# A ConvNeXt V2 block on one core: x turned by the DMA, the convolution cut into 32x32 tiles, a third of its result copied out by VectorE

## The chip, the core and the metric

The kernel runs on one core of one Trainium2 chip. A core has a matrix engine (TensorE, in the profile PE, with its weight loads as PEld), three elementwise engines (VectorE = DVE, ScalarE = ACT, GpSimd = POOL), and a queue for transfers (SyncE = SP); sixteen DMA engines move data. Each engine works through its own list of instructions in order, and lists are tied together by semaphores. Matrix results land in PSUM, eight banks of 512 float32 columns on 128 partitions; everything else lies in SBUF, also 128 partitions. The metric is the device time of one execution in microseconds.

## The reference

```python
# x (1,512,512,96), dw (3,3,96), w1 (96,384), w2 (384,96), gamma/beta (384): bfloat16
for i in range(3):
    for j in range(3):
        out = out + xp[:, i:i+H, j:j+W, :] * dw[i, j]      # depthwise 3x3, xp is x with a border of zeros
h = layernorm(out)                                         # over the 96 channels, eps 1e-5
h = gelu(einsum('bhwc,ce->bhwe', h, w1))                   # 96 -> 384 channels
gx = sqrt((h * h).sum(axis=(1, 2)) + 1e-6)                 # one number per channel, over the whole image
nx = gx / (gx.mean(axis=-1) + 1e-6)
h = gamma * (h * nx) + beta + h
return x + einsum('bhwe,ec->bhwc', h, w2)                  # 384 -> 96 channels
```

The sum over the image stands between the two products: nothing of the output can be made before all of h has been seen. The kernel therefore makes two passes over the image.

## The kernel before

The image is cut into 128 blocks of four rows (GR = 4), 2048 pixels each.

**First pass.** One slot of the loop at L826 does one block's convolution and, some slots later, the same block's norm and product. For block b:
- `load_x` (L216, queue SP) brings the block in with 16 pixels and a pixel of overlap at either side in each partition; `turn_x` (L442, two VectorE transposes of 128x576) puts channels on partitions, in the ring `xT` of five blocks. It is called three slots ahead of use, the load four.
- `conv_taps` (L463) makes the 3x3 convolution as matrix products with diagonal weights `Wq`. The partitions of a third `i` of the channels hold four image rows of 32 channels; an instruction takes 64 partitions (two rows) and gives 32 (one output row), so a block is 72 matmuls of 511 or 512 columns, in three bursts of 24. In a burst, eight successive matmuls go to the eight different 64x32 parts of the array. The result lies in banks 4 to 6 (`Y3`); in some early slots in others (`spare`).
- `evac` (L496) copies it to SBUF (`y_bf`) with one ScalarE instruction of 1536 columns. The next block's first burst writes the same banks and has to wait for it.
- POOL squares `y_bf` and later multiplies it with the row of 1/sigma (`yn`); PE sums for the moments (`stage_stats`), SP writes `yn` to DRAM and reads it back as `ynT` with 96 channels on the partitions.
- `mlp_units` (L699) makes h for an older block in 12 pieces of 512 columns: PE multiplies with `w1p`, ScalarE applies gelu into `g`. A block has four quarters. In `cm_quads(b)` of them h has its channels on the partitions, and three VectorE BATCH_NORM_STATS2 per quarter gather the sum of squares. The other quarters have pixels on the partitions, and PE gathers the squares by twelve 128x128 products per quarter (`gram`). Blocks with q % 10 in (0, 3, 7) below 114 are *whole*: four quarters with channels on the partitions, and `g` is stored to DRAM by SP. The block after a whole one has two such quarters, the others three; the last sixteen that are neither whole nor held have two or one.

The order is written out by hand: every engine call goes through `InOrder`, which keeps program order, so an engine's list is the order of the source. A slot with a product reads: burst 0, units 0 to 2, squares, burst 1, `turn_x`, units 3 to 5, squares, gram, units 6 and 7, squares, burst 2, `evac`, gram, units 8 to 11 and the moments. SP's list in a slot: the load of x for four slots later, the read of `ynT`, four writes of `yn`, rows and broadcasts of 1/sigma, and one third of a stored `g`.

**Tail.** The last 14 blocks have only their products left (`mlp_tail`, L672).

**Second pass** (from the middle of L950 on). For every block, h is loaded, kept or made again; 16 products per quarter with the scaled `W2s` give the output, VectorE adds x (`stage_mm2`, L328), SP stores.

Of the kernel before, what the change touches and what calls it, by code (L numbers as in the profile page):

```python
# [8 lines left out]
ALU = mybir.AluOpType  # L9
# [3 lines left out]
GR = 4  # L13
# [43 lines left out]
def kernel(  # L57
# [42 lines left out]
    def cm_quads(q):  # L100
        if is_whole(q) or is_held(q):
            return NQ
        if q > HELD[0]:
            return 1
        return 2 if q >= NBLK - 16 or (q - 1) % 10 in WHOLE else 3
# [4 lines left out]
    def chans(i):  # L110
        return slice(i, 64, 2) if i < 2 else slice(64, 96)
# [4 lines left out]
    def quad(flat_ap, t):  # L116
        return flat_ap.rearrange("p r (t g m) -> p t g r m", t=NQ, m=MB)[:, t]

    def quad_out(flat_ap):
        return flat_ap.rearrange("p (g r m) -> p g r m", r=GR, m=MB)  # L120
# [20 lines left out]
    Wq = consts.tile([128, NI, 3, GR, 32], bf16, name="Wq")  # L141
# [41 lines left out]
    SL = PXP + 2  # L183
    with ExitStack() as p1:
# [25 lines left out]
        xinpool = pc.enter_context(tc.tile_pool(name="xin", side="right", bufs=4))  # L210
        xins = {}

        def shift(h, j):
            return 1 if (h, j) == (0, GR - 1) else -1 if (h, j) == (1, 0) else 0

        def load_x(b):  # L216
            t = xinpool.tile([128, SL, C], bf16, name="xin")
            off = x.offset + b * GR * W * C
            rows = lambda p0, p1, s0, s1: (
                t[p0:p1, s0:s1, :].rearrange("p g c -> p (g c)"),  # L220
                bass.AP(x.tensor, off + (p0 * PXP - 1 + s0) * C, [[PXP * C, p1 - p0], [1, (s1 - s0) * C]]))
            if b == 0:
                pool.memset(t[0:1, 0, :], 0.0)
                parts = [(16, 128, 0, SL), (0, 16, 1, SL), (1, 16, 0, 1)]
            elif b == NBLK - 1:
                pool.memset(t[96:128, SL - 1, :], 0.0)
                parts = [(0, 112, 0, SL), (112, 128, 0, SL - 1), (112, 127, SL - 1, SL)]
            else:
                parts = [(0, 128, 0, SL)]
            for part in parts:  # L230
                o, i_ = rows(*part)
                sp.dma_start(out=o, in_=i_)
            xins[b] = t

        Wd = gpool.tile([128, NQ, NCH, QW], bf16, name="g")[:].rearrange("p t j w -> p (t j w)")[
            :, :NI * 9 * 32].rearrange("p (i k c) -> p i k c", i=NI, k=9)
# [8 lines left out]
        act.activation(out=Wq[:].rearrange("p i d j c -> p (i d j c)").rearrange("p (a w) -> p a w", a=3),  # L245
                       in_=zrow[:, None, :NI * GR * 32].to_broadcast([128, 3, NI * GR * 32]), func=ACTF.Identity)
# [8 lines left out]
        xtpool = pc.enter_context(tc.tile_pool(name="xt", side="right", bufs=1))  # L255
# [6 lines left out]
        NXT = 5  # L262
        xt_ring = []
        xt_all = xtpool.tile([128, NXT, NI, SL * MB], bf16, name="xT")
        for i in range(NXT):
            xt_ring.append(xt_all[:, i])
        assert NXT * NI * SL * MB >= NQ * NCH * QW
        g_over = xt_all[:].rearrange("p x i s -> p (x i s)")[:, :NQ * NCH * QW].rearrange(
            "p (t j w) -> p t j w", t=NQ, j=NCH)
# [32 lines left out]
        def cm_unit(g, ynt, t):  # L302
            U = banks3()
            for j in range(NCH):
                pe.matmul(quad_out(U[:, j, :]), lhsT=w1p[:, j * 128:(j + 1) * 128],
                          rhs=quad(ynt[:], t), start=True, stop=True)
            act.activation(out=g[:, t, :, :], in_=U, func=ACTF.Gelu_apprx_tanh)

        def px_unit(g, ynt, t):
            Uf = banks3().rearrange("p k w -> p (k w)")  # L310
            for r in range(GR):
                c = r * E
                while c < (r + 1) * E:
                    sz = min((r + 1) * E - c, W - c % W)
                    pe.matmul(Uf[:, c:c + sz], lhsT=ynt[:, r, t * 128:t * 128 + 128],
                              rhs=w1p[:, c - r * E:c - r * E + sz], start=True, stop=True)
                    c += sz
            act.activation(out=g[:, t, :, :].rearrange("p j w -> p (j w)"), in_=Uf, func=ACTF.Gelu_apprx_tanh)
# [9 lines left out]
        def stage_mm2(n, q):  # L328
            g, xb = grp[q]["g"], grp[q]["xb"]
            GQ = QW // 128  # L330
            o_sb = late.o.tile([128, PXP, C], bf16, name="o_sb")
            for sub in range(NSUB):
                O = out_bank()
                for gl_ in range(GPS):
                    gg = sub * GPS + gl_
                    for j in range(NCH):
# [3 lines left out]
                dve.tensor_tensor(out=o_sb[:, sub * GPS:(sub + 1) * GPS, :], in0=O,  # L340
                                   in1=xb[:, sub * GPS:(sub + 1) * GPS, :], op=ALU.add)
# [57 lines left out]
        n = 0  # L399
        for h in range(2):  # L400
            for j in range(GR):
                for q in (2 * h, 2 * h + 1):
                    a = q + GR * shift(h, j) - j + 1
                    if 0 <= a < 3:
                        n += 1
                        o, i_ = Wq[32 * q:32 * q + 32, :, :, j, :], Wd[32 * q:32 * q + 32, :, 3 * a:3 * a + 3, :]
                        if n % 2:
                            act.activation(out=o, in_=i_, func=ACTF.Identity)
                        elif n % 4:
                            dve.tensor_copy(out=o, in_=i_)  # L410
                        else:
                            pool.tensor_copy(out=o, in_=i_)

# [28 lines left out]
        def turn_x(b):  # L442
            xin = xins.pop(b)
            t = xt_ring[b % NXT]
            pairs = t[:, 0:2, :].rearrange("p i s -> p (i s)").bitcast(f32)
            dve.transpose(out=pairs.rearrange("p (g m) -> p g m", m=MB),
                          in_=xin[:, :, 0:64].bitcast(f32))
            dve.transpose(out=t[:, 2, :].rearrange("p (g m) -> p g m", m=MB), in_=xin[:, :, 64:96])

        def x_rows(b, p0, p1, i, c0, n):  # L450
            t = xt_ring[b % NXT]
            if i == 2:
                return t[p0:p1, 2, c0:c0 + n]
            return t[p0:p1, 0:2, :].rearrange("p i s -> p (i s)").rearrange(
                "p (s e) -> p s e", e=2)[:, c0:c0 + n, i]

# [6 lines left out]
        def conv_taps(b, spare):  # L463
# [6 lines left out]
            for n in range(3):  # L470
                mms.append([(h, j, (n + h) % NI, dx) for dx in (0, -1, 1) for j in range(GR) for h in range(2)])
            flat = [m for ms in mms for m in ms]
            first = {}
            last = {}
            for n, (h, j, i, dx) in enumerate(flat):
                first.setdefault((i, j), n)
                last[i, j] = n

            def burst(n, fence=True):
                k = sum(len(ms) for ms in mms[:n])  # L480
                for h, j, i, dx in mms[n]:
                    src = b + shift(h, j)
                    o0, o1 = max(0, -dx), W - max(0, dx)
                    pe.matmul(
                        Y[i][32 * j:32 * j + 32, o0:o1],
                        lhsT=Wq[64 * h:64 * h + 64, i, dx + 1, j, :],
                        rhs=x_rows(src, 64 * h, 64 * h + 64, i, MB * (1 + dx) + o0, o1 - o0)
                        if 0 <= src < NBLK else zrow[64 * h:64 * h + 64, o0:o1],
                        start=first[i, j] == k,
                        stop=last[i, j] == k,  # L490
                    )
# [207 lines left out]
        def mlp_units(b):  # L699
# [5 lines left out]
            def cm_mm(dst, j, t):  # L705
                pe.matmul(quad_out(dst), lhsT=w1p[:, j * 128:(j + 1) * 128], rhs=quad(yt[:], t), start=True, stop=True)

            def unit(bank, n):
# [10 lines left out]
                while c < end:  # L719
# [4 lines left out]
                    else:  # L724
# [3 lines left out]
                        col = (cm_quads(b) + t) * 128  # L728
                        pe.matmul(Uf[:, c - c0:c - c0 + sz], lhsT=yt[:, r, col:col + 128], rhs=w1p[:, e0:e0 + sz],
# [93 lines left out]
        turn_x(0)  # L823
        turn_x(1)
        turn_x(2)
        for s in range(last_slot + 1):  # L826
# [34 lines left out]
            elif not mlp:  # L861
                if s + 3 < NBLK:
                    turn_x(s + 3)
# [21 lines left out]
            else:  # L885
# [10 lines left out]
                if s + 3 < NBLK:  # L896
                    turn_x(s + 3)
# [100 lines left out]
    with p2:  # L998
        def out_part(q, o_sb, sub):
# [3 lines left out]
                    "(p g) c -> p g c", g=PXP)[:, sub * GPS:(sub + 1) * GPS],  # L1003
                in_=o_sb[:, sub * GPS:(sub + 1) * GPS])
# [47 lines left out]
```

## Time and profile before

| | us |
|---|---|
| median of 3 runs | 1489.95 (1483.42 to 1490.06) |
| the profiled execution: time / span of the profile | 1482.67 / 1480.8 |
| start and first slots | 0 to 113 |
| first pass, a product in every slot | 113 to 884 |
| last 14 products | 884 to 980 |
| end of the sums, second pass | 980 to 1481 |

Granted TensorE clock: 0.994 of full. The page gives each engine's busy share, then the span in 40 slices, the DMA queues, the chain that ended last, and groups of like instructions. A group's line reads: source line (most are that of the helper, L35), engine, operation, output and inputs by the program's names, partitions x elements, how many | busy time together, mean duration of one | idle time of the engine ahead of them and what ended it. As instructions of one engine overlap, mean times count can exceed the busy time. A timeline's line is start, length of the merged group, engine, operation, and in brackets the idle time ahead of it.

### The profile page before, as it was taken

The page shows a single profiled execution, that of the slowest core. Times are in us where ns is not written, and L with a number is a line of the kernel's source. Part 1 is how long each engine was busy: PE and PEld are TensorE (multiplying, and loading weights), DVE is VectorE, ACT ScalarE, POOL GpSimd, SP SyncE. Part 2 cuts the span into 40 slices and gives each one's busy share as a digit, 9 for nine tenths or more (in the row PEclk, how much of TensorE's full clock was granted, in tenths as well). Part 3 has the DMA queues.
Part 4 walks back from the last instruction along what each step waited for, and adds up shares of the span by engine and source line. Part 5 has one row for each costly group of instructions (what it writes and reads, how often), then busy time and mean ns, then how long its engine had stood idle before and what let it go on. Part 6 is the DMA issues. An engine that isn't in the chain of part 4 may idle for free.

```text
span 1480.8 us, 54225 instructions
## 1 busy us (share of the span) xinstructions
PE 1391.3 (94%) x23125; PEld 810.4 (55%) x23125; DVE 1182.0 (80%) x2135; ACT 1414.4 (96%) x1595; POOL 1300.3 (88%) x922
## 2 busy tenths in 40 slices
PE   8888999999999999999999997789999999999998
PEld 3434444444444444444444445467777777776776
DVE  7849989999999999999999987965555555555555
ACT  7888989999999999999999999999999999999997
POOL 3459889998998999998999987569999999999997
PEclk9999999999999999999999999999999999999999
DMA  5568788788888888888888866669999999999997
GB/s 180 179 205 255 241 253 280 228 271 260 260 248 264 258 264 255 276 253 254 263 258 266 263 216 195 195 225 409 366 359 402 417 416 413 419 410 417 411 412 282
DMA packets 167768, 433.08 MB, mean 292 GB/s; under 512 B 31558, under 2 KB 81318, under 8 KB 163046
## 3 DMA queue, kind: packets, MB, share of 16 engines
q1 hardware_dynamic: 151284, 326.04, 66.3%
q0 software_dynamic: 14880, 103.43, 17.6%
q8 instruction: 181, 2.97, 0.8%
q14 instruction: 61, 0.50, 0.1%
q10 hardware_dynamic: 1362, 0.15, 0.1%
HBM read 273.30 MB, written 156.22 MB: 290 GB/s over the span
## 4 chain that ended last, share of the span: by engine, by line
PE 30%; ACT 24%; DMA 19%; POOL 13%; DVE 6%; issue 4%; SPq 4%; POOLq 0%; ACTq 0%; DVEq 0%
PE PS L35 30%; ACT g L35 16%; DMA out_dram<-o_sb 9%; POOL yn L35 6%; ACT y_bf L35 5%; POOL ysq L35 5%; SPq L35 4%; DMA yn_dram<-yn 3%; DVE bst L35 3%; DMA xin<-in_x_dram 2%; DMA rbc<-r_dram 2%; DMA ynT<-yn_dram 1%; DMA g_dram<-g 1%; DVE o_sb L35 1%; ACT xT L35 1%
## 5 line engine op out<-in xcount | busy, mean ns | idle before, releaser
L35 ACT ACTIVATE g<-PS 128x512 bf16<-128x512 f32 (+2 forms) x1062 | 727.7, 864 | 16.5 <-PE PS L35 15.6
L35 DVE BATCH_NORM_STATS2 bst<-g 128x6 f32<-128x512 bf16 x1110 | 671.3, 672 | 35.4 <-ACT g L35 34.5
L35 PE MATMUL PS<-ynT,w1p 128*128 128x512 bf16 x2181 | 609.6, 381 | 23.6 <-ACT g L35 5.4
L35 ACT ACTIVATE gr<-PS 128x1536 bf16<-128x1536 f32 x360 | 498.5, 1459 | 18.8 <-PE PS L35 13.8
L35 POOL TENSOR_TENSOR yn<-y_bf,rbc 128x1536 bf16<-128x1536 bf16 x126 | 391.3, 3108 | 77.3 <-ACT rbc L35 21.9
L35 DVE TENSOR_TENSOR o_sb<-PS,xb 128x384 bf16<-128x384 f32 x512 | 277.3, 556 | 227.0 <-PE PS L35 190.1
L324 POOL TENSOR_TENSOR xb<-xr,B2c 128x1536 f32<-128x1536 bf16 x118 | 368.1, 3133 | 4.3 <-DVE o_sb L35 2.0
L35 PE MATMUL PS<-xT,Wq 64*32 64x511 bf16 (+1 forms) x9198 | 340.5, 389 | 26.2 <-ACT y_bf L35 8.1
L35 POOL TENSOR_TENSOR ysq<-y_bf 128x1536 bf16<-128x1536 bf16 x114 | 313.6, 2752 | 12.8 <-ACT y_bf L35 12.8
L35 PEld LDWEIGHTS <-w1p 128*128 128x128 bf16 x2181 | 171.6, 98 | 222.0 <-issue 133.4
L35 PEld LDWEIGHTS <-gr 128*128 128x128 bf16 x4296 | 212.1, 98 | 68.9 <-issue 12.0
L35 PE MATMUL PS<-W2s,gr 128*128 128x96 bf16 x4224 | 223.5, 206 | 8.2 <-DVE o_sb L35 8.0
L35 PEld LDWEIGHTS <-Wq 64*32 64x32 bf16 x9216 | 111.9, 90 | 193.3 <-issue 145.9
L35 ACT ACTIVATE y_bf<-PS 128x1536 bf16<-128x1536 f32 (+2 forms) x135 | 199.4, 1482 | 17.4 <-PE PS L35 13.3
L35 DVE STREAM_TRANSPOSE xT<-xin 128x576 f32<-128x576 f32 (+1 forms) x256 | 181.4, 748 | 8.1 <-DMA xin<-in_x_dram 8.1
L35 PEld LDWEIGHTS <-g 128*128 128x128 bf16 x1704 | 104.9, 98 | 86.3 <-issue 54.3
L35 PE MATMUL PS<-w1p,ynT 128*128 128x256 bf16 (+2 forms) x822 | 125.8, 273 | 8.0 <-ACT xT L35 3.2
L35 PE MATMUL PS<-g 128*128 128x128 bf16 x1464 | 122.6, 220 | 2.9 <-DVE PS L35 2.6
L35 PEld LDWEIGHTS <-gl 128*128 128x128 bf16 x1680 | 82.8, 98 | 26.8 <-issue 5.0
L35 PE MATMUL PS<-W2s,gl 128*128 128x96 bf16 x1680 | 89.5, 206 | 3.4 <-DVE o_sb L35 3.2
L35 PEld LDWEIGHTS <-ynT 128*128 128x128 bf16 x822 | 64.1, 97 | 31.5 <-issue 13.7
L279 POOL DMA_DIRECT2D xr<-in_x_dram x115 | 63.7, 555 | 14.2 <-POOL xb L324 14.2
(105 smaller groups left out, 576.5 us busy)
## 6 DMA issues: line engine op xcount, KB each, us to landing
xin<-in_x_dram SPq DMA_DIRECT2D x126, 432.0 KB
g_dram<-g SPq DMA_DIRECT2D x105, 512.0 KB
gl<-g_dram POOLq DMA_DIRECT2D x35, 1536.0 KB, 11.3
yn_dram<-yn SPq DMA_DIRECT2D x512, 96.0 KB
ynT<-yn_dram SPq DMA_DIRECT2D x128, 384.0 KB
out_dram<-o_sb SPq DMA_DIRECT2D x127, 384.0 KB
xr<-in_x_dram POOLq DMA_DIRECT2D x123, 384.0 KB, 6.9
ynT<-yn_dram SPq DMA_DIRECT2D x85, 512.0 KB
```

Source lines behind the costliest of these rows:

```text
L35: r = f(*a, **k)
L279: pq.dma_start(out=xr[:], in_=x[0, r0:r0 + GR].rearrange("r w c -> (r w) c").rearrange("(p g) c -> p g c", g=PXP))
L324: pq.tensor_tensor(out=xb[:], in0=grp[q]["xr"][:], in1=bias[:, None, :].to_broadcast([128, PXP, C]), op=ALU.add)
```

## The change

Six things, all in the first pass but the fourth.
1. x is loaded by a DMA that transposes (2-byte elements, 128 x 1536 to 128 x 12 x 128), straight into one ring of six blocks; the loads with overlap, the VectorE transposes and the copies of the weights at the start go. An element's partition is now given by its channel within 32 and by q % 4 with q = 3 (w mod 16) + i for column w and third i; the row and the rest of the column run along the free dimension. A quarter of a block is the pixels with one value of w mod 4.
2. The convolution takes 32 partitions and gives 32. Each of the nine taps is 12 matmuls of 512 columns on 12 of the sixteen 32x32 parts of the array. With dx of -1 or 1 one of the four column groups has its neighbour in another 16-pixel piece: its 512 columns are cut into 384 and 124, two matmuls on the same part of the array, one right behind the other, three such pairs per tap. For dx = -1 the pair stands first of the four of a third, for dx = 1 last. Where the ring wraps (every sixth block, above or below) each of a tap's matmuls is cut once more. In all 17892 matmuls of the convolution stand where 9216 did.
3. The bursts are now one dx each, with all three dy: 36, 45 and 45 matmuls.
4. The quarter of the product and of the output is one contiguous run on the product's side, and every fourth pixel in the second pass' addition and in the last block's four stores.
5. ScalarE copies out two thirds (1024 columns) and VectorE one (512).
6. The 34 blocks after a whole one have three quarters with channels on the partitions in place of two.

```diff
--- before
+++ after
@@ cm_quads @@
-        return 2 if q >= NBLK - 16 or (q - 1) % 10 in WHOLE else 3
+        return 2 if q >= NBLK - 16 else 3
@@ chans, quad @@
-        return slice(i, 64, 2) if i < 2 else slice(64, 96)
+        return slice(32 * i, 32 * i + 32)
-        return flat_ap.rearrange("p r (t g m) -> p t g r m", t=NQ, m=MB)[:, t]
+        return flat_ap[:, t, :]
@@ weights of the convolution @@
-    Wq = consts.tile([128, NI, 3, GR, 32], bf16, name="Wq")
+    Wd = consts.tile([128, NI, 9, 32], bf16, name="Wd")
@@ load_x @@
-        xinpool = pc.enter_context(tc.tile_pool(name="xin", side="right", bufs=4))
+        NXT = 6
+        xtpool = pc.enter_context(tc.tile_pool(name="xt", side="right", bufs=1))
+        xt = xtpool.tile([128, GR, NI, NXT * 128], bf16, name="xT")
         def load_x(b):
-            t = xinpool.tile([128, SL, C], bf16, name="xin")
...
-                sp.dma_start(out=o, in_=i_)
-            xins[b] = t
+            c = b % NXT * 128
+            sp.dma_start(out=xt[:, :, :, c:c + 128].rearrange("p k a s -> p (k a) s"),
+                         in_=x[0, b * GR:(b + 1) * GR].rearrange("r w c -> (r w c)").rearrange(
+                             "(p e) -> p e", p=128), transpose=True)
@@ stage_mm2 @@
-                dve.tensor_tensor(out=o_sb[:, sub * GPS:(sub + 1) * GPS, :], in0=O,
-                                   in1=xb[:, sub * GPS:(sub + 1) * GPS, :], op=ALU.add)
+                dve.tensor_tensor(out=o_sb[:, sub::NQ, :], in0=O, in1=xb[:, sub::NQ, :], op=ALU.add)
@@ setup: the loop that copies Wd into Wq (6 copies on ACT, 3 on DVE, 3 on POOL) goes, and turn_x with its calls @@
-            dve.transpose(out=pairs.rearrange("p (g m) -> p g m", m=MB),
-                          in_=xin[:, :, 0:64].bitcast(f32))
-            dve.transpose(out=t[:, 2, :].rearrange("p (g m) -> p g m", m=MB), in_=xin[:, :, 64:96])
@@ conv_taps @@
-            for n in range(3):
-                mms.append([(h, j, (n + h) % NI, dx) for dx in (0, -1, 1) for j in range(GR) for h in range(2)])
+            for dx in (0, -1, 1):
+                mm = []
+                for dy in (0, -1, 1):
+                    runs = []
+                    for r in range(GR):
+                        row = b * GR + r + dy
+                        if 0 <= row < H:
+                            at_ = row % (NXT * GR) * MB
+                            if runs and runs[-1][1] + (r - runs[-1][0]) * MB == at_:
+                                runs[-1][2] += 1
+                            else:
+                                runs.append([r, at_, 1])
+                    for r, at_, nr in runs:
+                        o = slice(r * MB, (r + nr) * MB)
+                        for i in range(NI):
+                            for sx in range(GR):
+                                wrap = not 0 <= sx + dx < GR
+                                q = NI * ((sx + dx) % GR) + i
+                                ko, ki = slice(0, GR), slice(0, GR)
+                                if wrap:
+                                    ko, ki = (slice(1, GR), slice(0, GR - 1)) if dx < 0 else (
+                                        slice(0, GR - 1), slice(1, GR))
+                                yo = Y[i][32 * sx:32 * sx + 32, :].rearrange("p (k s) -> p k s", k=GR)
+                                xi = xt[32 * (q % 4):32 * (q % 4) + 32, :, q // 4, :]
+                                w = Wd[32 * (q % 4):32 * (q % 4) + 32, i, 3 * (dy + 1) + dx + 1, :]
+                                mm.append(((i, sx), w, yo[:, ko, o], xi[:, ki, at_:at_ + nr * MB]))
+                                if wrap:
+                                    k0, k1 = (0, GR - 1) if dx < 0 else (GR - 1, 0)
+                                    m0, m1 = (1, 0) if dx < 0 else (0, 1)
+                                    mm.append(((i, sx), w,
+                                               yo[:, k0, o].rearrange("p (r m) -> p r m", m=MB)[:, :, m0:m0 + MB - 1],
+                                               xi[:, k1, at_:at_ + nr * MB].rearrange(
+                                                   "p (r m) -> p r m", m=MB)[:, :, m1:m1 + MB - 1]))
+                mms.append(mm)
@@ evac @@
-                    act.activation(out=y[:, 2, :], in_=Ub[:, 0, :], func=ACTF.Identity)
+                    dve.tensor_copy(out=y[:, 2, :], in_=Ub[:, 0, :])
-                    act.activation(out=y[:], in_=Y3, func=ACTF.Identity)
+                    act.activation(out=y[:, 0:2, :], in_=Y3[:, 0:2, :], func=ACTF.Identity)
+                    dve.tensor_copy(out=y[:, 2, :], in_=Y3[:, 2, :])
@@ out_part (last block only) @@
-                    "(p g) c -> p g c", g=PXP)[:, sub * GPS:(sub + 1) * GPS],
-                in_=o_sb[:, sub * GPS:(sub + 1) * GPS])
+                    "(p g) c -> p g c", g=PXP)[:, sub::NQ],
+                in_=o_sb[:, sub::NQ, :])
```

More of the change, by code (lines that the diff above doesn't have):

```diff
@@ L116, in quad @@
     def quad(flat_ap, t):
-        return flat_ap.rearrange("p r (t g m) -> p t g r m", t=NQ, m=MB)[:, t]
-    def quad_out(flat_ap):
-        return flat_ap.rearrange("p (g r m) -> p g r m", r=GR, m=MB)
+        return flat_ap[:, t, :]
     def yn_src(q):
@@ L182 @@
     p2 = ExitStack()
-    SL = PXP + 2
     with ExitStack() as p1:
@@ L209 @@
         pc = p1.enter_context(ExitStack())
-        xinpool = pc.enter_context(tc.tile_pool(name="xin", side="right", bufs=4))
-        xins = {}
-        def shift(h, j):
-            return 1 if (h, j) == (0, GR - 1) else -1 if (h, j) == (1, 0) else 0
-        def load_x(b):
-            t = xinpool.tile([128, SL, C], bf16, name="xin")
[L218 to L231, printed above, removed]
-                sp.dma_start(out=o, in_=i_)
-            xins[b] = t
-        Wd = gpool.tile([128, NQ, NCH, QW], bf16, name="g")[:].rearrange("p t j w -> p (t j w)")[
-            :, :NI * 9 * 32].rearrange("p (i k c) -> p i k c", i=NI, k=9)
+        NXT = 6
+        xtpool = pc.enter_context(tc.tile_pool(name="xt", side="right", bufs=1))
+        xt = xtpool.tile([128, GR, NI, NXT * 128], bf16, name="xT")
+        assert GR * NI * NXT * 128 >= NQ * NCH * QW
+        g_over = xt[:].rearrange("p k a s -> p (k a s)")[:, :NQ * NCH * QW].rearrange(
+            "p (t j w) -> p t j w", t=NQ, j=NCH)
+        def load_x(b):
+            c = b % NXT * 128
+            sp.dma_start(out=xt[:, :, :, c:c + 128].rearrange("p k a s -> p (k a) s"),
+                         in_=x[0, b * GR:(b + 1) * GR].rearrange("r w c -> (r w c)").rearrange(
+                             "(p e) -> p e", p=128), transpose=True)
         zrow = consts.tile([128, W], bf16, name="zrow")
@@ L244 @@
         act.activation(out=warm[:], in_=warm[:], func=ACTF.Gelu_apprx_tanh)
-        act.activation(out=Wq[:].rearrange("p i d j c -> p (i d j c)").rearrange("p (a w) -> p a w", a=3),
-                       in_=zrow[:, None, :NI * GR * 32].to_broadcast([128, 3, NI * GR * 32]), func=ACTF.Identity)
         for b in range(2, min(4, NBLK)):
@@ L254 @@
         cen = consts.tile([C, 128], bf16, name="cen")
-        xtpool = pc.enter_context(tc.tile_pool(name="xt", side="right", bufs=1))
         ypool = pc.enter_context(tc.tile_pool(name="ybf", side="right", bufs=13))
@@ L261 @@
         ynpool = pc.enter_context(tc.tile_pool(name="yn", side="right", bufs=3))
[L262 to L269, printed above, removed]
         NS = BATCH * GR * NG
@@ L304, in cm_unit @@
             for j in range(NCH):
-                pe.matmul(quad_out(U[:, j, :]), lhsT=w1p[:, j * 128:(j + 1) * 128],
+                pe.matmul(U[:, j, :], lhsT=w1p[:, j * 128:(j + 1) * 128],
                           rhs=quad(ynt[:], t), start=True, stop=True)
@@ L314, in px_unit @@
                     sz = min((r + 1) * E - c, W - c % W)
-                    pe.matmul(Uf[:, c:c + sz], lhsT=ynt[:, r, t * 128:t * 128 + 128],
+                    pe.matmul(Uf[:, c:c + sz], lhsT=ynt[:, t, r * 128:r * 128 + 128],
                               rhs=w1p[:, c - r * E:c - r * E + sz], start=True, stop=True)
@@ L330, in stage_mm2 @@
             GQ = QW // 128
+            assert GQ == GPS and NSUB == NQ
             o_sb = late.o.tile([128, PXP, C], bf16, name="o_sb")
@@ L398 @@
                               in1=Ud[:, i, :, None].to_broadcast([128, 9, 32]), op=ALU.mult)
[L399 to L412, printed above, removed]
         for i in range(NI):
@@ L440, in setup_rest @@
             dve.tensor_copy(out=gam[:], in_=gam_bf[:])
[L442 to L445, printed above, removed]
-            dve.transpose(out=pairs.rearrange("p (g m) -> p g m", m=MB),
-                          in_=xin[:, :, 0:64].bitcast(f32))
-            dve.transpose(out=t[:, 2, :].rearrange("p (g m) -> p g m", m=MB), in_=xin[:, :, 64:96])
[L450 to L455, printed above, removed]
         ybf, ysq, yns, rbcs, msts, rns, rts = ({} for _ in range(7))
@@ L469, in conv_taps @@
             mms = []
-            for n in range(3):
-                mms.append([(h, j, (n + h) % NI, dx) for dx in (0, -1, 1) for j in range(GR) for h in range(2)])
-            flat = [m for ms in mms for m in ms]
+            for dx in (0, -1, 1):
[32 more added lines that the diff above has]
+                mms.append(mm)
@@ L473, in conv_taps @@
             first = {}
             last = {}
-            for n, (h, j, i, dx) in enumerate(flat):
-                first.setdefault((i, j), n)
-                last[i, j] = n
+            for n, m in enumerate(m for mm in mms for m in mm):
+                first.setdefault(m[0], n)
+                last[m[0]] = n
             def burst(n, fence=True):
[L480 to L491, printed above, removed]
+                k = sum(len(mm) for mm in mms[:n])
+                for to, w, o, i_ in mms[n]:
+                    pe.matmul(o, lhsT=w, rhs=i_, start=first[to] == k, stop=last[to] == k)
@@ L705, in cm_mm @@
             def cm_mm(dst, j, t):
-                pe.matmul(quad_out(dst), lhsT=w1p[:, j * 128:(j + 1) * 128], rhs=quad(yt[:], t), start=True, stop=True)
+                pe.matmul(dst, lhsT=w1p[:, j * 128:(j + 1) * 128], rhs=quad(yt[:], t), start=True, stop=True)
             def unit(bank, n):
@@ L727, in unit @@
                         t, r = divmod(k, GR)
-                        col = (cm_quads(b) + t) * 128
-                        pe.matmul(Uf[:, c - c0:c - c0 + sz], lhsT=yt[:, r, col:col + 128], rhs=w1p[:, e0:e0 + sz],
+                        pe.matmul(Uf[:, c - c0:c - c0 + sz], lhsT=yt[:, cm_quads(b) + t, r * 128:r * 128 + 128], rhs=w1p[:, e0:e0 + sz],
                                   start=True, stop=True)
@@ L822 @@
         busy(FILL[1])
-        turn_x(0)
-        turn_x(1)
-        turn_x(2)
         for s in range(last_slot + 1):
@@ L861 @@
             elif not mlp:
-                if s + 3 < NBLK:
-                    turn_x(s + 3)
                 for f in taps:
@@ L895 @@
                 spread_out()
-                if s + 3 < NBLK:
-                    turn_x(s + 3)
                 unit(3, 1)
```

## The prediction

> **What bounds the kernel now.** I read the busy time by stage first, because shares over the whole span mix four stages.
>
> ```profile
> core 0: us, PE busy (x) PEld busy (x) DVE busy (x) ACT busy (x) POOL busy (x), PEclk, DMA share, GB/s
> ...
> 113.00:884.00 771.00, 733.45 (x13265) 358.67 (x13263) 752.99 (x1290) 757.18 (x1075) 718.34 (x532) 0.99 0.82 256
> ...
> 980.00:1481.00 501.00, 485.73 (x7113) 360.50 (x7111) 275.07 (x508) 475.39 (x344) 472.81 (x280) 1.00 0.99 391
> ```
>
> The second pass (last line) has its DMA engines full, and nothing that it transfers changes. The stage to look at is 113 to 884: there the convolution's results are copied out every 7.03 us, so it is 771/7.03 = 110 slots. In one slot ACT is busy 6.9 us, DVE 6.9, PE 6.7, POOL 6.55 and the DMA 5.8: four engines lie within 6%, and whichever grows by more than its few tenths of slack sets the slot. So I took the groups of the quiet middle of this stage (57 slots):
>
> ```profile
> L35 DVE BATCH_NORM_STATS2 bst<-g 128x6 f32<-128x512 bf16 x507 | 306.4, 671 | 1.5 <-ACT g L35 1.1
> ...
> L35 ACT ACTIVATE g<-PS 128x1024 bf16<-128x1024 f32 x169 | 188.7, 1116 | 2.3 <-PE PS L35 1.4 <-ACT g L35 1.0
> ...
> L35 ACT ACTIVATE y_bf<-PS 128x1536 bf16<-128x1536 f32 x57 | 89.5, 1570 | 0.0
> ...
> L35 DVE STREAM_TRANSPOSE xT<-xin 128x576 f32<-128x576 f32 x57 | 43.4, 761 | 0.0
> ...
> L35 DVE STREAM_TRANSPOSE xT<-xin 128x576 bf16<-128x576 bf16 x57 | 41.9, 736 | 0.0
> ```
>
> DVE gives a BATCH_NORM 306.4/507 = 0.60 us and the turning of x (43.4 + 41.9)/57 = 1.5 us a slot. ACT takes 1.57 us for the copy, of which the timeline shows 1.33 before the next piece starts (599.10 to 600.43). Last, PE in order of time over one slot:
>
> ```profile
> 600.72 0.88 PE L35 MATMUL PS<-xT,Wq 64*32 64x512 bf16 x24 [0.16 <-ACT y_bf L35]
> 601.73 0.82 PE L35 MATMUL PS<-ynT,w1p 128*128 128x512 bf16 x3
> 602.48 0.86 PE L35 MATMUL PS<-xT,Wq 64*32 64x512 bf16 x24
> 603.27 0.85 PE L35 MATMUL PS<-ynT,w1p 128*128 128x512 bf16 x3
> 603.97 0.50 PE L35 MATMUL PS<-g 128*128 128x128 bf16 x6
> 604.30 0.60 PE L35 MATMUL PS<-w1p,ynT 128*128 128x384 bf16 x4
> 604.83 0.88 PE L35 MATMUL PS<-xT,Wq 64*32 64x512 bf16 x24
> 605.64 0.51 PE L35 MATMUL PS<-g 128*128 128x128 bf16 x6
> ...
> 607.75 0.65 PE L35 MATMUL PS<-xT,Wq 64*32 64x512 bf16 x16
> ```
>
> PE goes from group to group without a hole, except 0.16 us before the first burst and 0.13 after it (601.60 to 601.73). PE has about 0.3 us to spare in 7.03, no more; anything added to its list beyond that lengthens the slot. Two prices follow. Three whole-array matmuls of 512 columns take 0.82 us where one takes 0.383, so the columns stream at (0.82 - 0.383)/2 = 0.22 us for 512, or 0.165 for 384 and 0.053 for 124. And 24 matmuls on eight parts of the array take 0.88 where one takes 0.39: three waves, 0.22 to 0.245 apart, the eight of a wave side by side.
>
> **The change, part by part.**
>
> *Convolution on PE.* A tap is now one wave of 12 matmuls on 12 parts. The burst with dx = 0 has three taps, so three waves, as each burst has today: cost 0. In the other two bursts a column group's 512 columns are cut into 384 and 124 on the same part. The second cannot start until the first has streamed, 0.165 us. What do the matmuls behind it do, which go to free parts? If they pass, a tap stays one wave (384 + 124 are 508 columns) and the cost is 0. If they wait, each of the three pairs of a tap holds the list 0.165 us, a tap takes 0.495 and three taps 1.485. For dx = -1 the last matmuls then start 1.485 after the first where it is 0.44 today: +1.05. For dx = 1 the pair stands last, and its 124 columns end at 1.485 + 0.053 = 1.54 where 0.66 is today's end: +0.88. Together +1.9 us a block. No row shows a matmul held by its own part of the array, so 0 and 1.9 are the ends. The nearest row is the hole at 601.60: the three product matmuls stand waiting for their bank, and the 24 of the next burst, whose banks and x have long been there, do not pass them but come at 602.48. That is a list taken strictly in order, so I take 1.9. The additional cuts at the ring's ends share out the same columns and I cost them at nothing, hidden in the same waves.
>
> [...] The trace shows parts side by side, and no overtaking.
>
> *Third quarter in 34 blocks.* It removes 204 pixel-major pieces (34 x 4 rows of 384 columns, 0.165 each, 22 us) and 408 gram products (six take 0.50 where one takes 0.22: 0.056 each, 23 us) and adds 102 whole matmuls (22 us): -23 us of PE, -0.2 a slot. On DVE it adds 102 x 0.60 = 61 us, +0.56 a slot.
>
> *Copying out.* ACT loses 512 of 1536 columns. The pieces of g cost (188.7/169 - 200.8/338) = 0.52 us for 512 columns more in mean busy time, the copy itself 1.33/3 = 0.44: I take -0.44, leaving ACT at 6.5. DVE gains a 128x512 copy from PSUM; the nearest rows are the BATCH_NORM of the same width (0.60) and the 128x384 addition from PSUM of the second pass (0.556). I take 0.6. It is also a new wait: the next block's first burst waits for DVE as well, whose copy is queued behind the slot's BATCH_NORMs; behind it on DVE stand those of the third quarter, for which nothing but a buffer of g waits. DVE's sum is 6.9 - 1.5 + 0.6 + 0.56 = 6.6 us, under the new slot by nearly 2 us, which hides the copy; in the three slots of ten after a whole block it has twelve BATCH_NORMs and about 7.9 us, still just hidden. If that cover goes I would pay about 0.3 us in 33 slots, 10 us.
>
> *Loading x.* The load waits for PE's last burst of the slot before (the ring entry is read there) where it waited for a DVE transpose. Behind it on SP stand the read of ynT, the writes of yn and the rest of the slot. At the shown slot SP reached the load at 608.58 and the burst ended at 605.71, so the wait has ended and costs nothing. In DMA time, packets in the trace's records took 10.6 ns for 64 bytes, 46 for 1024 undisturbed and 56 in the mean; the load now takes 128 packets of 3456 bytes at 172 ns, 1.4 us of sixteen engines' time. The transposing load's inner run is 128 elements, 256 bytes; between those rows by size a packet is 18 to 20 ns, and 1536 of them 1.8 us. That transposing itself is free is not shown. If rows break into 64-byte pieces, 6144 x 10.6/16 = 4.1 us; if into single 4-byte ones (9.4 ns), 58 us; the low end is today's 1.4. I take 1.8, nearest to the row length in the code: DMA 5.8 + 0.4 = 6.2 us a slot, hidden under 8.4.
>
> *Start, tail, second pass.* The weight copies at the start (ACT's last at 7.9 us, the first burst at 8.1) and the first transposes go; two transposing loads must land instead. I take 0 with 3 us either way. The second pass' additions read runs of 96 numbers as before; DVE is half idle there. 0.
>
> *Sum.* The slot becomes 7.03 + 1.9 - 0.2 - 0.3 (PE's holes, since ACT, which ended them, is ahead now) = 8.4: +1.4 x 110 = +154 us. The 18 slots before 113 us take 3.5 to 9 us each, and the burst lies there on the way from copy to moments to norm; between 0 and 1.9 apiece I take 1.4: +25. Together +179 on the profiled execution's 1482.7, 1662; that run is 0.5% under the median of the three shown (1489.95), next to the lowest.
>
> **The rivals.**
>
> *Matmuls overtake.* Then PE needs 6.7 - 0.2 = 6.5, ACT 6.5, POOL 6.55 and DVE 6.6; the slot would fall to between 6.7 and 7.03, since DVE's copy in the loop takes away the freedom of its queue. At 6.87, -0.16 x 110 = -18 us: 1465 (1447 to 1485). For it: parts run side by side today. Against it: the hole at 601.60. It decides as soon as less than 0.5 us of the 1.9 is paid (6.53 + 0.5 is today's slot).
>
> *The transposing load is slow.* Other transfers take 5.8 - 1.4 = 4.4 us a slot, so DMA sets the slot when a block's transpose takes over 4.0 us. At 5.5, between the 64-byte bound and 32-byte pieces (12288 at 9.4 ns, 7.2 us), the slot is 9.9: +1.5 more in 128 slots, 1850. The same would follow if SP, whose issues fill some 5.3 us of the slot, took over 3.5 us to issue one. For it: nothing in the trace transposes in a DMA. Against it: DMA has 2 us of room. [...]
>
> **How the numbers follow.** Measurement here tells about 0.5%. In order: 0.56; overtaking: 0.21; slow transpose: 0.23. The likeliest's own range is 1620 (none of the early slots pay, 0.15 us more of slack is found) to 1715 (no hole is regained, early slots pay in full, DVE's copy is late). For eight in ten the range must reach down into the overtaking case, to 1460 (leaving 0.05 of it out), and up to 1740 (leaving 0.15 of the slow transpose). Faster by over 0.5% is most of the overtaking case, 0.17; within, 0.05; slower, the other two, 0.78.
>
> **What would show it.** In the changed kernel's slot the dx = -1 and dx = 1 bursts should last about 1.9 us on PE beside 0.9 for dx = 0, copies out of PSUM should come every 8.4 us, PE should be the one engine without holes, and ACT, DVE and POOL should wait for PE. If those bursts last 0.9, the first rival holds. If PE waits for xT, or DMA is at 1.0 in this stage, the second. The prediction is wrong too if PE waits for DVE's copy in most slots.

## The result and the profile after

The changed kernel takes 1578.54 us (median of four runs, 1574.57 to 1585.46) where the kernel before takes 1490.0: 1.0611 times as long, with a 95% interval of 1.0564 to 1.0658. The forecast was 1662 in a range of 1460 to 1740. The sign and the range hold; the size is half of what was forecast. As the runs show, the one term that made the forecast is not there, while others, costed at nothing or nearly so, are.

The profiled execution took 1574.57 us (span 1572.8). By stage, cut where the convolution's results are copied out for the 20th and the last time and where the second pass begins; first the changed kernel, then the same cuts of the kernel before:

```profile
0.00:128.60 128.60, 105.03 (x3365) 61.55 (x3366) 67.22 (x167) 80.50 (x97) 56.58 (x69) 0.95 0.79 162
128.60:975.40 846.80, 762.04 (x20127) 428.10 (x20125) 742.40 (x1279) 726.95 (x1073) 715.75 (x539) 0.98 0.97 229
975.40:1060.30 84.90, 67.12 (x619) 42.43 (x617) 74.00 (x150) 82.85 (x65) 51.34 (x31) 1.00 0.64 198
1060.30:1573.00 512.70, 492.18 (x7188) 364.67 (x7186) 277.96 (x516) 482.64 (x349) 472.43 (x280) 1.00 0.97 382
```

```profile
0.00:113.10 113.10, 97.25 (x2051) 43.49 (x2052) 77.59 (x182) 91.58 (x111) 52.74 (x71) 0.98 0.62 189
113.10:883.70 770.60, 733.04 (x13262) 358.49 (x13260) 752.59 (x1289) 756.78 (x1074) 717.98 (x531) 0.99 0.82 256
```

The columns are PE, PEld, DVE, ACT and POOL busy (and instructions), granted clock, DMA share, GB/s. I call the stretch of the second row, 108 slots, the steady stage. Of the 92 us between the spans 76 lie in the 108 slots between the cuts (7.14 us a slot became 7.84), 15 in the slots before, -4 in the tail and +5 in the second pass. In the steady stage no engine is the bound any more: PE's share fell from 95% to 90%, ACT's from 98 to 86, DVE's from 98 to 88, POOL's from 93 to 85. Only the DMA's rose, 0.82 to 0.97, and it moves less. The granted clock is 0.980 where it was 0.993; by an estimate from these two, if PE had set the pace all the time that would be 11 us of the 76 at most.

The groups that answer to those shown before (400 to 800 us; 51 slots here):

```profile
L35 DVE BATCH_NORM_STATS2 bst<-g 128x6 f32<-128x512 bf16 x501 | 305.8, 676 | 45.0 <-ACT g L35 44.9
...
L35 PE MATMUL PS<-xT,Wd 32*32 32x512 bf16 x4058 | 143.7, 386 | 19.2 <-DVE y_bf L35 14.5 <-issue 4.0
...
L35 ACT ACTIVATE y_bf<-PS 128x1024 bf16<-128x1024 f32 x51 | 54.4, 1067 | 4.2 <-PE PS L35 4.0
...
L35 DVE CAST y_bf<-PS 128x512 bf16<-128x512 f32 x51 | 34.1, 668 | 0.4 <-PE PS L35 0.4
```

DVE now waits 45 us for ACT, and PE's convolution waits for DVE's copy. PE in order of time, in a slot without trouble:

```profile
609.79 0.94 PE L35 MATMUL PS<-xT,Wd 32*32 32x512 bf16 x36
610.83 0.82 PE L35 MATMUL PS<-ynT,w1p 128*128 128x512 bf16 x3
611.58 0.89 PE L35 MATMUL PS<-xT,Wd 32*32 32x384 bf16 x45
612.40 0.82 PE L35 MATMUL PS<-ynT,w1p 128*128 128x512 bf16 x3
613.05 0.50 PE L35 MATMUL PS<-g 128*128 128x128 bf16 x6
613.39 0.59 PE L35 MATMUL PS<-ynT,w1p 128*128 128x512 bf16 x2
613.91 0.89 PE L35 MATMUL PS<-xT,Wd 32*32 32x512 bf16 x45
...
615.73 0.40 PE L35 MATMUL PS<-rowsel,y_bf 128*128 128x4 bf16 x10
616.47 0.20 PE L35 MATMUL PS<-rowsel,y_bf 128*128 128x4 bf16 x2 [0.34 <-issue]
```

All three bursts last 0.9 us, those of 45 matmuls too, where the forecast said 1.9: matmuls do pass one that waits for its part of the array. The starts of single matmuls in the burst at 611.58 show it (from the trace's records; the three of 124 columns are issued 2nd, 7th and 12th of the first 15):

```
384 columns   611.576  611.593  611.610
512 columns   611.583 .586 .590   611.600 .603 .606   611.616 .620 .623
124 columns   611.750  611.766  611.783
```

Twelve start within 47 ns, the three cut-off pieces 0.174 us after the 384 columns in front of them. The one issued second starts thirteenth: between different parts of the array, PE does not keep strictly to the order of its list.

Only where the ring's end cuts a burst to 60 matmuls is it longer, for instance:

```profile
640.17 1.05 PE L35 MATMUL PS<-xT,Wd 32*32 32x512 bf16 x60
```

The last two lines of the list of one slot show something else. Ten of twelve like matmuls, then a stop, then the other two, with no semaphore between them. Who waited for whom on PE between 113 and 880 us, in the changed kernel and in the kernel before:

```profile
PE PS L35 <- issue: 32.1, 42, 3.1
PE PS L35 <- DVE y_bf L35: 27.5, 24, 3.3
PE PS L35 <- ACT g L35: 3.3, 6, 1.2
```

```profile
PE PS L35 <- ACT y_bf L35: 3.8, 19, 0.7
PE PS L35 <- DVE PS L35: 1.9, 3, 1.6
PE PS L35 <- ACT g L35: 1.1, 1, 1.1
```

The numbers are us in total, times, the longest; "issue" means that PE waited for nothing the profile shows. These stops follow a pattern. One DMA queue, q8 of the page, of kind instruction, brings pieces of 16384 bytes, 181 in the kernel before and 245 in the changed one. 256 times that is 46336 and 62720; PE's list (matmuls and weight loads) has 46250 and 62582 records. By an estimate from these counts a piece holds 256 of PE's instructions. Counted along that list, the distances between the stops are near whole multiples of 256: in the changed kernel from 73 us on 255, 255, 254, 255, 508 and 509 records. And of the changed kernel's stops over 0.5 us marked "issue" between 113 and 880 us all 24 end 1.2 to 1.7 us after such a piece has landed, a stretch that covers about a tenth of that time.

I call these fetch holes: over 0.3 us from one start on PE (weight loads included) to the next, the second 1.15 to 1.8 us after a piece landed. Up to the end of the first pass's products the kernel before has 67 of them, 28 us in all, and the changed one 113, 86 us. Part of that is chance, ordinary gaps that happen to lie there: with the landing times moved by 1.5 to 4 us either way the same count gives 24 us in the mean (19 to 32) in the kernel before and 33 (27 to 39) in the changed one. So nearly all of the 28 us is chance. Beyond chance there are 4 us before and 53 after, in the steady stage alone 3 and 40, each give or take 5.

### The profile page after: what moved, and what is told of

Its sections match the earlier page's. It is cut to its first block, busy times and chain, and to the rows that moved or that the text cites. A ratio compares the mean times of both kernels' runs of the same rounds, so it can differ in the third digit from the quotient of the medians.

```text
span 1572.8 us, 70544 instructions
## 1 busy us (share of the span) xinstructions
PE 1426.4 (91%) x31291; PEld 896.7 (57%) x31291; DVE 1161.6 (74%) x2110; ACT 1372.9 (87%) x1581; POOL 1296.1 (82%) x917
## 5 line engine op out<-in xcount | busy, mean ns | idle before, releaser
L35 DVE BATCH_NORM_STATS2 bst<-g 128x6 f32<-128x512 bf16 x1212 | 738.7, 676 | 111.6 <-ACT g L35 111.2
L35 PE MATMUL PS<-ynT,w1p 128*128 128x512 bf16 x2283 | 644.7, 383 | 28.8 <-ACT g L35 8.4
L35 PE MATMUL PS<-xT,Wd 32*32 32x512 bf16 x17892 | 397.2, 338 | 74.3 <-issue 35.2
L35 PEld LDWEIGHTS <-Wd 32*32 32x32 bf16 x17892 | 226.8, 90 | 271.9 <-issue 248.5
L35 ACT ACTIVATE y_bf<-PS 128x1024 bf16<-128x1024 f32 x128 | 136.0, 1063 | 46.7 <-PE PS L35 46.4
L35 DVE CAST y_bf<-PS 128x512 bf16<-128x512 f32 x128 | 85.9, 671 | 48.9 <-PE PS L35 48.9
L35 PEld LDWEIGHTS <-g 128*128 128x128 bf16 x1296 | 79.8, 98 | 41.7 <-issue 17.7
L35 PE MATMUL PS<-w1p,ynT 128*128 128x384 bf16 (+2 forms) x618 | 96.5, 272 | 7.7 <-ACT xT L35 3.2
L35 PE MATMUL PS<-g 128*128 128x128 bf16 x1056 | 89.4, 221 | 1.7 <-DVE PS L35 1.3
L35 PEld LDWEIGHTS <-y_bf 128*128 128x128 bf16 x1536 | 56.4, 96 | 20.9 <-issue 11.2
```

Of the source, the lines that this page charges most:

```text
L35: r = f(*a, **k)
```

## The experiments

After the result the theory was: PE has no more columns to stream than before, and the slot grew through the DMA engines (filled by the transposing load), through DVE's copy standing in PE's loop behind DVE's queue, or through PE running out of instructions. Ratios are to the kernel before on the same chip; the changed kernel's is 1.0611. Times by stage are of one execution each and less exact than the ratios: from chip to chip the median of the kernel before lay between 1479 and 1490 us.

**ScalarE copies out everything again.**

```diff
-                    act.activation(out=y[:, 0:2, :], in_=Y3[:, 0:2, :], func=ACTF.Identity)
-                    dve.tensor_copy(out=y[:, 2, :], in_=Y3[:, 2, :])
+                    act.activation(out=y[:], in_=Y3, func=ACTF.Identity)
```

> The changed kernel with one part undone: ScalarE copies out all three chunks again. Theory: the slot grew from 7.03 to 7.84 us for two reasons, VectorE's copy in PE's loop (late in the one slot of ten that has three BATCH_NORM_AGGREGATEs ahead of it, 10.5 us long) and DMA engines filled by the transposing load. Then the slots of 10.5 us go, the others stay near 7.5: 1578 - 33 = about 1545. Rival A, VectorE's copy is all of it: 1495 to 1510. Rival B, the DMA is all of it, long slots included: 1575 or more, since ScalarE gets 0.44 us a slot more.

Measured: 1559.99 us, ratio 1.0542 (1.0501 to 1.0583). By the ratios that is a gain of some 10 us, less than the theory's 33 and far from rival A. The mean slot is 7.65 us; the slots at every tenth place are no longer the long ones (7.7 us in the mean, 9.95 in the changed kernel), but others of up to 12 us stand elsewhere.

**The load as a plain DMA in the same pieces.**

```diff
-                         in_=x[0, b * GR:(b + 1) * GR].rearrange("r w c -> (r w c)").rearrange(
-                             "(p e) -> p e", p=128), transpose=True)
+                         in_=x[0, b * GR:(b + 1) * GR].rearrange("r w c -> (r w c)").rearrange(
+                             "(p e s) -> p e s", p=128, s=128))
```

> The changed kernel with the load as a plain DMA that writes the same ring in the same 1536 pieces of 256 bytes, not turned; so the convolution works on wrong pixels and the output isn't the reference's. If small pieces fill the DMA engines: unchanged, 1570 to 1585, packets of 256 bytes again near 2.8 us a block. If it is the turning (packets of 256 bytes have a median of 18 ns but a mean of 29): 1.8 us a block, DMA share under 0.9 in the first pass, and 1578 - 40 = about 1540. If the DMA does not matter at all: 1578 whatever the packets take.

Measured: 1559.99 us, ratio 1.0534 (1.0488 to 1.058). The DMA share in the steady stage:

```profile
129.00:958.80 829.80, 756.70 (x20127) 426.66 (x20125) 740.44 (x1278) 724.96 (x1074) 718.15 (x540) 0.98 0.85 233
```

A block's packets take 1.79 us of sixteen engines in place of 2.79 (mean over all 128 blocks), and the share falls to 0.85, as the forecast's 1.8 had it for pieces of that size. So turning costs 1.0 us of DMA a block: in the changed kernel the packets of 256 bytes have a median of 18 ns, as here, but 1.3% take over 100 ns and hold 54 of the 142 us that they take between 400 and 800 us. Yet by the ratios the time fell by some 11 of the expected 40 us only: full DMA engines are not what the whole waits for.

**The aggregates behind the copy.**

```diff
                 conv(2)
                 if evac:
                     evac()
+                    combine_owed()
...
-            for b in get("combine"):
-                combine(b)
+            owed_agg.extend(get("combine"))
```

> The changed kernel with the three BATCH_NORM_AGGREGATEs of a filled group put behind VectorE's next copy of the convolution instead of ahead of it; nothing else moves. Theory: the slots of 10.5 us (one in ten, 3 us over their neighbours) shrink to the others' 7.5, 1578 - 33 = 1545 to 1550. Rival B, the DMA makes them: 1578.

Measured: 1561.32 us, ratio 1.0549 (1.0507 to 1.0592). In the mean over the steady stage the slots at every tenth place fell from 9.95 to 8.0 us and the next ones rose from 7.4 to 8.3. By the ratios some 9 of the expected 28 to 33 us came: what is taken from one wait is in good part lost to the next. Each of the three gains so far, 0.6 to 0.8 points, is hardly larger than the intervals, which touch that of the changed kernel.

**The pieces of 124 columns last.**

```diff
-                                    mm.append(((i, sx), w,
+                                    late_mm.append(((i, sx), w,
...
+                        mm += late_mm
```

> The changed kernel with the three matmuls of 124 columns of a tap moved behind the tap's other twelve, so that none stands right behind the matmul that fills its part of the array. The prediction's step (a held matmul holds those behind it, 1.9 us a block) would make this faster by more than 100 us. The trace of the changed kernel shows bursts of 0.85 to 0.89 us, so matmuls for other parts pass: 1578, no change beyond 0.5%.

Measured: 1574.55 us, ratio 1.0658 (1.06 to 1.0716), the same as the changed kernel. The order within a tap costs nothing, so the forecast's step falls by time as well as by the trace.

**The kernel before with twice the matmuls.**

```diff
-                    pe.matmul(
-                        Y[i][32 * j:32 * j + 32, o0:o1],
+                    for c0, c1 in ((o0, 256), (256, o1)):
+                        pe.matmul(
+                            Y[i][32 * j:32 * j + 32, c0:c1],
```

> The kernel before with each of its 9216 convolution matmuls cut into two of half the columns on the same part of the array, with its own weight load: 18432 matmuls, nearly the changed kernel's 17892, and nothing else. Columns and waves are the same, so by columns alone PE's time stays and the ratio is 1.00. Theory C, PE runs out of instructions (holes of 0.5 to 3.3 us inside runs of instructions that wait for nothing, 41 us between 200 and 880 in the changed kernel, 1 us in the kernel before): with so many the list is fetched too late here as well, ratio 1.015 to 1.03.

Measured: 1534.87 us, ratio 1.0361 (1.0323 to 1.0399), above the range that the theory gave. Nothing but the number of instructions (matmuls and their weight loads) was changed, and the same holes open; two neighbouring groups of one burst, and PE's waits between 113 and 880 us:

```profile
215.50 0.42 PE L35 MATMUL PS<-xT,Wq 64*32 64x256 bf16 x8
217.36 0.87 PE L35 MATMUL PS<-xT,Wq 64*32 64x256 bf16 x40 [1.44 <-issue]
```

```profile
PE PS L35 <- issue: 26.4, 38, 1.6
PE PS L35 <- ACT g L35: 3.0, 5, 1.5
```

Fetch holes went from 67 (28 us) to 110 (71 us), beyond chance from 4 to 46 us: 42 of the 50 us by which the span grew. In the steady stage alone the time grew by 30 us and the holes beyond chance by 31; between 113 and 880 us all 20 stops over 0.5 us marked "issue" end 1.2 to 1.7 us after a piece has landed, as in the changed kernel. A reserve: bursts last a little longer too (0.92 us by the profile's modelled ends, where it was 0.87), 0.15 us a slot, an estimated 16 us if PE's slack hid none of it. The holes stand here at a DMA share of 0.79.

**The turned x into a buffer that nothing reads** (the convolution of this and the next two and of the last run reads zeros). In these four runs POOL first clears the ring, which takes 4 us, and the first copy starts at 15 to 16 us in place of 10.6: some 5 us, 0.3 points, of their times come from that.

```diff
-            sp.dma_start(out=xt[:, :, :, c:c + 128].rearrange("p k a s -> p (k a) s"),
+            xs = xspool.tile([128, GR * NI, 128], bf16, name="xs")
+            sp.dma_start(out=xs[:], in_=x[0, b * GR:(b + 1) * GR].rearrange("r w c -> (r w c)").rearrange(
...
```

> The changed kernel with the transposing load written to a scratch buffer that nothing reads (the convolution reads zeros, so the output isn't the reference's). DMA work stays, the load's wait for PE on the SP queue goes, and with it whatever stands behind it. Theory D, that wait is what costs (SP waits 96 us for PE between 400 and 800, 24 in all for POOL and PE before): ratio 1.03 or less. If the DMA's fullness or the fetch of instructions is the cause: 1.055 to 1.065.

Measured: 1588.65 us, ratio 1.0704 (1.0634 to 1.0774). Between 400 and 800 us SP waits 12 us for PE in place of 96, but the steady stage takes 848 us where the changed kernel takes 847. SP's wait for PE alone is not the cause; theory D falls in this setting.

**A plain load into that buffer.**

```diff
-            sp.dma_start(out=xt[:, :, :, c:c + 128].rearrange("p k a s -> p (k a) s"),
+            xs = xspool.tile([128, GR * NI * 128], bf16, name="xs")
+            sp.dma_start(out=xs[:], in_=x[0, b * GR:(b + 1) * GR].rearrange("r w c -> (r w c)").rearrange(
...
-                             "(p e) -> p e", p=128), transpose=True)
+                "(p e) -> p e", p=128))
```

> As the last, but the load a plain one of 128 runs of 3072 bytes: no wait for PE, and the DMA engines no fuller than in the kernel before (about 1.2 us a block, share 0.8). The convolution reads zeros. If DMA and SP's wait are the cause together: 1.02 or less (VectorE's copy left). If the fetch of instructions is the cause: 1.04 to 1.05.

Measured: 1572.77 us, ratio 1.063 (1.0582 to 1.0677). No theory said that: with the DMA engines no fuller than in the kernel before (0.76 in the steady stage) and SP's wait for PE down to 11 us, next to nothing is gained; the steady stage takes 837 us. What stands in the way is DVE's copy, as the next run shows. PE and DVE around one of the long slots of this run:

```profile
629.98 0.41 PE L35 MATMUL PS<-xT,Wd 32*32 32x512 bf16 x8
633.56 1.04 PE L35 MATMUL PS<-xT,Wd 32*32 32x512 bf16 x28 [3.17 <-DVE y_bf L35]
```

```profile
626.51 2.77 DVE L35 BATCH_NORM_AGGREGATE mv<-bst 128x2 f32<-128x192 f32 x3
629.19 3.60 DVE L35 BATCH_NORM_STATS2 bst<-g 128x6 f32<-128x512 bf16 x6
632.70 0.23 DVE L35 STREAM_TRANSPOSE rt<-rstd 128x64 bf16<-128x64 bf16 x1
632.85 0.66 DVE L35 CAST y_bf<-PS 128x512 bf16<-128x512 f32 x1
```

PE has done the first eight matmuls, into the two banks that ACT copies out, and stands for 3.17 us until DVE, which has three aggregates, six BATCH_NORMs and a transpose ahead of the copy, has copied the third bank.

**The same, and ScalarE copies out everything.** The edits of the last and of the first run together.

> The run with the plain load into scratch, and ScalarE copying out all three chunks. What is left of the change is the 32x32 convolution and the third quarters. If nothing but DMA, SP's wait and VectorE's copy made the kernel slower: 0.99 to 1.005 (ScalarE needs 7.0 us a slot again). If the fetch of instructions does: 1.025 to 1.04.

Measured: 1524.1 us, ratio 1.0295 (1.0243 to 1.0347). Now half of the loss is gone. The steady stage:

```profile
137.50:925.10 787.60, 722.88 (x19952) 430.27 (x20124) 680.59 (x1170) 761.14 (x1074) 708.67 (x537) 1.00 0.80 244
```

The mean slot is 7.29 us, and between 400 and 800 us PE waits no more than 0.5 us at a time for ACT. Fetch holes are 100, 65 us, beyond chance 34. The span is 41 us longer than that of the kernel before: 17 in the steady stage, where the holes beyond chance are 18 longer, and 24 in the slots before, of which some 5 are the clearing of the ring. That fits theory C.

**The kernel before with a third of its matmuls cut.**

```diff
+                    for c0, c1 in ((o0, 256), (256, o1)) if dx == 0 else ((o0, o1),):
```

> The kernel before with a third of its convolution matmuls (those with dx = 0) cut in two: 12288 in place of 9216, a third of the additional instructions of the full cut, which gave 1.036. Theory C (the list is fetched in pieces of 256 instructions, and PE stands where it has run through a piece faster than the next comes): more holes than before, fewer than with the full cut, ratio 1.008 to 1.02. If the cost of the full cut came from something else, such as a limit passed only at twice the number: 1.00.

Measured: 1488.85 us, ratio 1.0062 (1.0044 to 1.0079). The interval leaves a small cost, below the range given and a sixth of the full cut's for a third of the instructions. The loss grows faster than the number. Its holes can't be read from the trace: the profiled execution took 1479.04 us, the fastest of five and no slower than the kernel before. PE's "issue" waits between 113 and 880 us are 3.9 us there (26.4 with the full cut, none listed without), and the 82 fetch holes, 38 us, are 9 beyond chance.

**Plain load into the buffer, DVE's copy, aggregates late.** The edits of the seventh and of the third run together.

> Plain load into scratch, VectorE still copying a third, but the three BATCH_NORM_AGGREGATEs behind the copy. The neighbours are 1.063 (aggregates ahead of the copy) and 1.0295 (no copy on VectorE). If the aggregates ahead of the copy are what VectorE's copy costs (3.2 us of PE's waiting in one slot of ten, slots of 10.9 us): 1.03 to 1.04. If the queue of BATCH_NORMs is: 1.055 to 1.063.

Measured: 1556.71 us, ratio 1.0514 (1.049 to 1.0537). Between the two: the aggregates are 1.2 points of the 3.4 that DVE's copy costs here. The rest I put down to the ordinary queue ahead of it, which no run took away by itself.

The changed kernel and three of the runs make a table (ratio, and mean slot of the steady stage in us, where the kernel before has 7.14):

| | x turned into the ring | x plain, into a buffer nothing reads |
|---|---|---|
| DVE copies a third | 1.061, 7.84 | 1.063, 7.75 |
| ScalarE copies everything | 1.054, 7.65 | 1.0295, 7.29 |

Either edit alone gives 0.7 points or nothing, both give 3.2. The two causes lie over one another: a slot waits for whichever is later, and taking one away shows the other.

## Why the prediction was right and wrong

That the sign and the range held is luck. The mechanism that made the forecast was not there, and the time grew by others. By the signs the prediction set itself, bursts of 0.9 us spoke for its first rival and a DMA share near 1 for its second.

**Convolution on PE: wrong, and it was the whole forecast.** The step "I take 1.9", from "that is a list taken strictly in order", failed. The hole at 601.60 showed matmuls waiting for a semaphore, and the 24 behind them kept their order, from 602.48 on. A busy part of the array held only the matmuls meant for it: in the burst at 611.58 the three pieces of 124 columns came 0.174 us later, and twelve others started within 47 ns. The lower end of the bounds, 0, was the truth by columns, except at the ring's ends: those cuts were put at "nothing, hidden in the same waves", but a burst of 60 lasts 1.05 us where one of 45 takes 0.89 (and one of 48 0.98 for 0.85), 0.45 us in a third of the blocks. The larger additional cost is one that the section never looked for: it counted the columns of 17892 matmuls and not their instructions. Doubling the matmuls without a column more cost 3.6%, and the changed kernel with the load and the copy taken back, the third quarters left in, is 2.95% slower.

**Copying out: prices right, cover wrong.** ACT's copy takes 1.07 us for 1.57, DVE's 0.67 for the 0.6 assumed. The wait was named, with the queue in front of it, and priced at "10 us" at most, because DVE's sum left "nearly 2 us" a slot. A sum over a slot does not hide a wait inside it: the copy must be done by the time the next burst's third bank is due, and in the slot shown with the plain load PE stood 3.17 us for it. With the loads plain, DVE's copy is worth 3.4 points, about 50 us; in the changed kernel itself 0.7, since the other cause then takes its place. The aggregates, which come three at a time in one slot of ten, were left out of the step altogether.

**Loading x: the size was bounded, its effect not.** The packets took 2.79 us a block, between the 1.4 and the 4.1, against 1.8 taken; the plain run in the same pieces took 1.79, so the estimate by size was right and the turning itself was the gap. 393 KB in 2.79 us are 141 GB/s, beside other traffic. The DMA share of 0.97 was called hidden "under 8.4", a slot that never came. SP's wait for PE was costed at nothing; SP waited 96 us for PE between 400 and 800 where it was 12, but without the wait the time did not fall (1.070), so that cost is not shown.

**Third quarter.** Predicted at -0.2 us of PE a slot, hidden on DVE. It was not measured by itself and stays open.

**Start, tail, second pass.** First copy 1.5 us earlier, within the 3 us; the first slots cost 15 us where 25 were taken, but for other reasons, as fetch holes there went from 4.5 to 19 us. The second pass is 5 us longer, against 0, but the tail is 4 us shorter; from the last copy to the end both kernels take 597 us.

**Rivals.** "Matmuls overtake" was given 0.21 and was right on the mechanism, wrong in what follows, since it made PE's slot of 6.5 us the bound. "The transposing load is slow" came to 2.8 of the 4.0 us a block at which it was to set the slot, and still mattered. The time fell between the cases, inside the range, by causes that were no case's ground: instructions, and DVE's copy together with the load.

What stays open: why a piece of instructions comes late, if that is what the holes are, though its packet takes no longer (1.13 us in the mean up to 900 us, in both kernels); whether, once ScalarE copies, it is the full DMA engines or SP's wait for PE that makes the 2.5 points between 1.054 and 1.0295, since the plain load took both away; and the third quarters. The steady stages of the runs at 1.054 and 1.0295 are 38 us apart, and the holes beyond chance are 42 us in the one and 21 in the other. So about half of that difference would be fetch holes; this speaks for the DMA engines rather than SP, but no run shows it.

## What to carry to other kernels

Count instructions beside columns: cutting the same matmuls in two cost 3.6% here at an unchanged number of columns, cutting a third of them 0.6%, so a finer tiling can have a price in the length of the engine's list. Look at the queue ahead of a copy that a loop waits for, and not only at the engine's share of busy time: DVE was 88% busy in the steady stage, and its copy, behind three aggregates, six BATCH_NORMs and a transpose, held PE for 3.17 us. Where two causes lie over one another, undo them together as well as one by one; each alone showed 0.7% or nothing of what was 3%.

## What the hardware showed that was not expected

- Matmuls for free parts of the array pass one whose part is busy: in the burst at 611.58 twelve start within 47 ns, the three issued among them 0.174 us after the 384 columns ahead of them, for which the prediction's estimate was 0.165 us.
- In the changed kernel PE stands for up to 3.1 us in the middle of a run of instructions without a wait that the profile shows; from 73 us on such places are 255, 255, 254, 255, 508 and 509 records apart, and between 113 and 880 us all 24 stops over 0.5 us marked "issue" end 1.2 to 1.7 us after a 16384-byte piece has landed. With 9216 and 18432 convolution matmuls in otherwise the same kernel, such holes beyond chance sum to 4 and 46 us.
- The transposing load in pieces of 256 bytes took 2.79 us of sixteen DMA engines for 393 KB, a plain one in the same pieces 1.79; between 400 and 800 us 1.3% of the transposing load's packets took over 100 ns and hold 54 of its 142 us.
